# First K by the plain queue beside first Q by the cast queue, and weights in two column halves, in a planned attention and FFN kernel

## The chip, the cores and the metric

The kernel runs on one core of a Trainium2 chip. The core has five engines that work side by side, each through its own list of instructions in a fixed order: TensorE (PE, matmul), VectorE (DVE), ScalarE (ACT), GpSimd (POOL) and SyncE (SP). SP, ACT and POOL also issue DMAs, which 16 DMA engines shared by all of them carry out. The metric is the device time of one execution in microseconds (us), the median over several runs. All runs and traces here are of one core.

## The reference

Block-sparse attention over 4 batches and 8 heads, 768 positions, 64 wide, and then a gated FFN over the 3,072 tokens:

```python
scores = q @ k.T / sqrt(64)            # per batch and head, 768 x 768
mask   = |block_i - block_j| <= 1, first and last block row and column,
         and 3 sampled key blocks for each query block   # blocks of 32
attn   = softmax(where(mask, scores, -1e9))
x      = (attn @ v), heads side by side                  # 3072 x 512
gate   = sigmoid(x @ w_gate)                             # 512 x 1536
out    = (gate * (x @ w_val)) @ w_out                    # 1536 x 512
```

All inputs are float32 in HBM (the sampled blocks are integers), and the output is float32. The kernel computes in float16 with float32 sums.

## The kernel before

The work is cut into 12 tiles n of 256 query tokens: batch b = n // 3 and chunk c = n % 3. The 8 heads go in 4 pairs p. For each (n, p) there are three score groups of 256 keys each: `attend` (L546) makes the transposed scores on PE (L560), the exponential on ACT (L575, 128 x 1024 in one instruction), and the mask. Tile 0 adds the mask as a bias on PE (the other half of L560); later tiles multiply by a 0/1 mask on DVE (L583). Then 24 matmuls with V (L598) give the values and, through a column of ones, the row sums. DVE takes the reciprocal (L606) and scales (L609), and the result x is transposed, for the first three tiles on PE (L634, copied by DVE at L639), for later ones by a DMA of SP (L622).

When all four pairs of a tile are there, `ffn` (L648) runs over 12 blocks f of 128 hidden columns: 4 matmuls with w_gate and 4 with w_val (L660), a tanh on ACT (L679), and a product on DVE (L686). After the 12 blocks, L704 multiplies with w_out, ACT or DVE evacuates y (L721, L717), and SP stores it (L726).

Inputs of batch 0 come by POOL's queue, which casts float32 to float16 on the way: `load_half` (L396), and `turn_pe` (L402) transposes K and Q on PE (L410), DVE copying the result (L414). Q is loaded for all heads at once, first the third that tile 0 needs (`qc0`), and last the other two thirds (`qc12`). The order is K0, qc0, K1, V0, K2, V1, K3, V2, V3, qc12. The weights follow in POOL's queue: gate and value in column blocks 0-256, 256-512, 512-1024 and 1024-1536 (L457), then w_out in three pieces (L466). Batches 1 to 3 come by SP's queue as float32: `load` (L357, L362) for K, Q and V of one pair; ACT or DVE casts them (`cast_qk`, L391 or L393; `cast_v`, L382 or L384), and `turn_dma` (L418) has SP transpose K and Q (L424). Three staging buffers each for K, Q and V (`ks`, `qs`, `vs`) bound how far these loads run ahead. Those of batch 1 wait for the second piece of w_out.

Nothing of this order is dynamic on the chip. A planner, class `Plan`, takes every operation with an engine (or two, for casts), a duration, its buffers and a priority, plays the whole kernel through in Python with these durations, and at each step gives a free engine the ready operation of the lowest priority number. The order that comes out is what each engine's list holds. The planner knows DMAs by the line `dma_free = max(dma_free, now + 2.1) + o.dma`, landing 0.2 later. Where a DMA comes later on the chip than in the plan, the engine that stands in front of its data waits, and with it all that is behind it in its list. While PE has nothing to do in the plan before 22 us, it gets matmuls on zeros (L347, the "spin").

## Time and profile before

| | us |
|---|---|
| median of 5 runs | 302.55 |
| lowest and highest | 300.15 and 302.87 |
| the profiled execution, its own time | 300.15 |
| span of its trace | 298.4 |
| first exponential (L575) begins | 9.24 |
| first FFN matmul (L660) begins | 26.87 |
| last store begins after y of | 295.18 |
| PE, ACT, DVE busy | 288.8, 211.8, 192.6 |

The span is the time from the first to the last instruction; some 1.75 us of the execution's own time lie around it. The granted TensorE clock is full throughout. The profiled execution is the lowest of the five runs, so what is worked out from its trace is set against 300.15 first, and against the median after that.

DMAs from issue to landing, as the list of DMA issues gives them (the size is that of the destination; a casting DMA reads twice as much):

| what | queue | KB | issue to landing, us |
|---|---|---|---|
| table e (issued at 0.74) | SP | 192 | 2.3 |
| K of pair 0 (issued at 1.24) | POOL | 192 | 4.0 |
| qc0 (issued at 2.04) | POOL | 256 | 4.7 |
| qc12 (issued at 7.89) | POOL | 512 | 9.6 |
| gate and value, 512 columns | POOL | 512 | 12.9 to 15.8 |
| w_out, three pieces | POOL | 512 | 16.9 to 19.3 |
| K, Q, V of batches 1 to 3 | SP | 384 | 5.4 to 5.6 (medians) |

How to read the profile: a row of the timeline has the start, the time from start to end, the engine, the source line, the operation, what it writes and reads, and how many instructions were merged; in brackets stands the idle time of the engine before it and what ended it. PEld is the load of weights into PE, beside the matmuls. PEq, SPq and the like are the sequencers, which issue DMAs and wait. The chain of waits is followed back from the last instruction; its rows have the start, the length and what decided in that time.

### The profile page before, as it was taken

The page shows a single profiled execution, that of the slowest core. Times are in us where ns is not written, and L with a number is a line of the kernel's source. Part 1 is how long each engine was busy: PE and PEld are TensorE (multiplying, and loading weights), DVE is VectorE, ACT ScalarE, POOL GpSimd, SP SyncE. Part 2 cuts the span into 40 slices and gives each one's busy share as a digit, 9 for nine tenths or more (in the row PEclk, how much of TensorE's full clock was granted, in tenths as well). Part 3 has the DMA queues.
Part 4 walks back from the last instruction along what each step waited for, and adds up shares of the span by engine and source line. Part 5 has one row for each costly group of instructions (what it writes and reads, how often), then busy time and mean ns, then how long its engine had stood idle before and what let it go on. Part 6 is the DMA issues. An engine that isn't in the chain of part 4 may idle for free.

```text
span 298.4 us, 8114 instructions
## 1 busy us (share of the span) xinstructions
PE 288.8 (97%) x3407; PEld 211.1 (71%) x3407; DVE 192.6 (65%) x448; ACT 211.8 (71%) x328; POOL 16.0 (5%) x25
## 2 busy tenths in 40 slices
PE   8898998999999899999999999999999999999995
PEld 6676874776687478578578677768768767778673
DVE  3769868788777687576667567756656756635230
ACT  1789795998887878788678578678578578434331
POOL 8750000000000000000000000000000000000000
PEclk9999999999999999999999999999999999999999
DMA  9999999999979957460210210120120120120101
GB/s 122 193 198 207 206 267 309 307 306 285 266 176 237 299 181 104 106 159 3 64 46 0 53 58 1 29 81 0 29 81 0 29 82 1 29 81 0 38 35 70
DMA packets 53420, 35.36 MB, mean 119 GB/s; under 512 B 32136, under 2 KB 50440, under 8 KB 53384
## 3 DMA queue, kind: packets, MB, share of 16 engines
q1 hardware_dynamic: 43248, 27.77, 35.7%
q0 software_dynamic: 10064, 7.08, 16.0%
q8 instruction: 26, 0.43, 0.7%
q14 instruction: 10, 0.08, 0.1%
q10 hardware_dynamic: 72, 0.01, 0.0%
HBM read 28.55 MB, written 6.29 MB: 117 GB/s over the span
## 4 chain that ended last, share of the span: by engine, by line
PE 74%; DMA 16%; POOL 3%; SPq 2%; ACT 2%; DVE 1%; issue 1%; POOLq 0%
PE psum L660 38%; PE psum L704 18%; PE psum L560 9%; PE psum L598 9%; DMA wo<-in_moe_w_out_dram 6%; DMA wv<-in_moe_w_val_dram 4%; DMA vs<-in_v_dram 3%; DMA ks<-in_k_dram 2%; SPq L362 1%; DMA qs<-in_q_dram 1%; ACT pt L575 1%; POOL k L398 1%; POOL q L398 1%; POOL qc L398 1%; DVE pt L583 0%
## 5 line engine op out<-in xcount | busy, mean ns | idle before, releaser
L575 ACT ACTIVATE pt<-psum 128x1024 f16<-128x1024 f32 x144 | 143.3, 1024 | 34.8 <-PE psum L560 34.7
L583 DVE TENSOR_TENSOR pt<-pt,mask 128x1024 f16<-128x1024 f16 x132 | 90.5, 690 | 49.2 <-ACT pt L575 48.9
L660 PE MATMUL psum<-x,wg 128*128 128x256 f16 x576 | 86.7, 273 | 1.2 <-DMA x<-x 0.8
L660 PE MATMUL psum<-x,wv 128*128 128x256 f16 x576 | 86.7, 273 | 0.0
L686 DVE SCALAR_TENSOR_TENSOR h<-tg,psum 128x256 f16<-128x256 f32 x144 | 56.6, 415 | 19.0 <-ACT tg L679 18.8
L679 ACT ACTIVATE tg<-psum 128x256 f32<-128x256 f32 x144 | 55.2, 388 | 16.9 <-PE psum L660 13.1
L704 PE MATMUL psum<-wo,h 128*128 128x512 f16 (+1 forms) x300 | 66.6, 371 | 0.0
L660 PEld LDWEIGHTS <-wv 128*128 128x128 f16 x576 | 53.7, 98 | 12.9 <-issue 7.1
L660 PEld LDWEIGHTS <-wg 128*128 128x128 f16 x576 | 54.8, 98 | 10.6 <-issue 3.5
L704 PEld LDWEIGHTS <-h 128*128 128x128 f16 x300 | 27.6, 98 | 30.7 <-issue 3.6
L560 PE MATMUL psum<-qT,kT 64*128 64x256 f16 x576 | 47.8, 271 | 1.5 <-ACT pt L575 1.5
L598 PEld LDWEIGHTS <-pt 128*128 128x128 f16 x1152 | 41.0, 97 | 5.0 <-issue 1.6
L598 PE MATMUL psum<-v,pt 128*128 128x65 f16 x1152 | 42.8, 193 | 0.5 <-DVE pt L583 0.4
L560 PEld LDWEIGHTS <-kT 64*128 64x128 f16 x576 | 23.5, 94 | 16.5 <-issue 13.4
L721 ACT ACTIVATE y<-psum 128x512 f32<-128x512 f32 (+1 forms) x21 | 12.1, 577 | 23.4 <-PE psum L704 21.7
L609 DVE TENSOR_TENSOR x<-psum,rz 128x256 f16<-128x256 f32 x48 | 20.3, 424 | 1.7 <-DVE rz L606 0.2
L606 DVE RECIPROCAL rz<-psum 128x4 f32<-128x4 f32 x48 | 8.5, 177 | 13.5 <-PE psum L598 13.1
L393 ACT CAST q<-qs 128x768 f16<-128x768 f32 x7 | 5.8, 832 | 5.1 <-DMA qs<-in_q_dram 5.1
L391 DVE CAST k<-ks 128x768 f16<-128x768 f32 x8 | 4.5, 557 | 4.4 <-DMA ks<-in_k_dram 4.4
L384 ACT CAST v<-vs 128x768 f16<-128x768 f32 x7 | 5.8, 834 | 1.3 <-PE psum L598 1.0
L560 PE MATMUL psum<-bias,e 64*128 64x256 f16 x48 | 6.4, 272 | 0.1
L532 DVE TENSOR_SCALAR mask<-psum 128x512 f16<-128x512 f32 x9 | 6.0, 685 | 0.3
(40 smaller groups left out, 70.8 us busy)
## 6 DMA issues: line engine op xcount, KB each, us to landing
out_dram<-y SPq DMA_DIRECT2D x23, 256.0 KB, 2.3
ks<-in_k_dram SPq DMA_DIRECT2D x12, 384.0 KB, 5.4
qs<-in_q_dram SPq DMA_DIRECT2D x12, 384.0 KB, 5.6
vs<-in_v_dram SPq DMA_DIRECT2D x12, 384.0 KB, 5.5
wo<-in_moe_w_out_dram POOLq DMA_DIRECT2D x3, 512.0 KB, 18.1
wg<-in_moe_w_gate_dram POOLq DMA_DIRECT2D x2, 512.0 KB, 14.3
wv<-in_moe_w_val_dram POOLq DMA_DIRECT2D x2, 512.0 KB, 14.9
k<-in_k_dram POOLq DMA_DIRECT2D x4, 192.0 KB, 5.5
```

What stands on the lines that cost most here:

```text
L398: landed[nm] = nc.gpsimd.dma_start(t(), src[nm][0][:, hs, js])
L560: nc.tensor.matmul(st()[:, hd, jj * CH : (jj + 1) * CH], l[r, 2 * tt + jj, :], m[r, 2 * c : 2 * c + 2, :], start=not (own and masked), sto ...
L575: lambda st=st, pt=pt: nc.scalar.activation(pt().rearrange("p h j q -> p h (j q)"), st(), AF.Exp, scale=SCALE),
L583: nc.vector.tensor_tensor(t, t, mask()[:, c, tt].unsqueeze(1).to_broadcast([128, 2, 512]), op=ALU.mult)
L598: nc.tensor.matmul(o()[:, 2 * jq + hd, 0:65], pts[j // 2]()[:, hd, j % 2, jq * 128 : jq * 128 + 128], v_[:, hd, j, 0:65], start=(j == 0), ...
L606: P.op("DVE", 0.2, lambda: nc.vector.reciprocal(rz(), o()[:, :, 64:65]), reads=[o], writes=[rz], prio=seq - 5)
L609: lambda: nc.vector.tensor_tensor(x16().rearrange("p j (h d) -> p (j h) d", d=64), o()[:, :, 0:64], rz().to_broadcast([128, 4, 64]), op=AL ...
L660: nc.tensor.matmul(t()[:, z : z + w], wt()[:, i, f * 128 : (f + 1) * 128], xT[g, i]()[:, 0:w], start=(i == 0), stop=(i == NP - 1),)
L679: lambda tg=tg, a=pair[0]: nc.scalar.activation(tg()[:, 0:w], a[0]()[:, a[1] : a[1] + w], AF.Tanh, scale=0.5),
L686: lambda tg=tg, a=pair[1], h_=h_: nc.vector.scalar_tensor_tensor(h_()[:, 0:w], tg()[:, 0:w], 1.0, a[0]()[:, a[1] : a[1] + w], op0=ALU.add, ...
L704: nc.tensor.matmul(py()[:, m], hts[g, f]()[:, tt * 128 : (tt + 1) * 128], wo()[:, f, m], start=(f == 0), stop=(f == NF - 1),)
L721: lambda py=py, y=y, m=m: nc.scalar.activation(y()[:, m], py()[:, m], AF.Copy, scale=0.5),
```

## The change

The change does the following.

- K of pair 0 of batch 0 is loaded by SP in float32, as SP's first DMA, ahead of the table e, and ACT casts it into a buffer of its own. The identity goes from SP's queue to ACT's.
- POOL's queue loads Q by pairs, whole, in the order of `FIRST`: Q0, K1, Q1, K2, Q2, V0, K3, Q3, V1, V2, V3. The transposes of Q still come in two parts, the third for tile 0 first and the rest before tile 1.
- Gate and value weights come in two halves of 768 columns.
- K, V and Q of pair 0 of batch 1 (the last entry of `HALF`) also come by POOL's casting queue, between the value weights and w_out, and are transposed on PE.
- SP's loads of batch 1 (now pairs 1 to 3) wait for the third piece of w_out instead of the second; a load also stands behind the transposes of earlier pairs (`turned`).
- The planner's constants for DMAs are others: 1.9 (SP, ACT) or 2.6 (POOL) to the first byte, 0.3 at the end, more per load, and a `slack` that is added to a landing (0.3 or 1.3 for casting loads, 1.5 for SP's loads). POOL begins at 0.55.
- Score groups of `attend` are kept in order (`scored`), and the building of the masks is tied to points in the attention (`behind`), with its DVE part at a lower priority number.

```diff
+EDGES = [0, 768, 1536]
+FIRST = [
+    ("q", 0), ("k", 1), ("q", 1), ("k", 2), ("q", 2), ("v", 0), ("k", 3), ("q", 3), ("v", 1), ("v", 2), ("v", 3),
+]
+HALF = [(0, 0), (0, 1), (0, 2), (0, 3), (1, 0)]
...
+        free["POOL"] = 0.55
...
-                    dma_free = max(dma_free, now + 2.1) + o.dma
-                    o.seen = dma_free + 0.2
+                    first = now + (2.6 if e == "POOL" else 1.9)
+                    if o.dma > 0.15:
+                        first = dma_free = max(dma_free, first) + o.dma
+                    o.seen = first + 0.3 + o.slack
...
+    P.op("ACT", 0.4, lambda: nc.scalar.dma_start(ident16(), id_h.ap()), writes=[ident16], prio=-88, dma=0.1)
...
-        writes=[e24], prio=-92, dma=0.5,
+        writes=[e24], prio=-94.5, dma=0.5,
...
-    P.op("SP", 0.5, lambda: nc.sync.dma_start(ident16(), id_h.ap()), writes=[ident16], prio=-91, dma=0.3)
...
+    def load_half(nm, b, p, prio, dur=0.72):
+        c = sb(f"{nm}16" if nm != "v" else "vh", [128, 2, NJ, 64], f16)
+        half16[nm, b, p] = stage[nm, b, p] = c
+        o = P.op(
+            "POOL", dur, lambda: nc.gpsimd.dma_start(c(), src[nm][b][:, 2 * p : 2 * p + 2]),
+            writes=[c], prio=prio, dma=1.28,
+        )
+        o.slack = 0.3 + b
+        return o
...
+    load("k", 0, 0, -95)
+    t, c = stage["k", 0, 0], one([128, 2, NJ, 64], f16, "k16_first")
+    half16["k", 0, 0] = c
+    P.op("ACT", 0.83, lambda t=t, c=c: nc.scalar.copy(c(), t()), reads=[t], writes=[c], prio=-67)
+    for i, (nm, p) in enumerate(FIRST):
+        last_in = load_half(nm, 0, p, -60 + i, 0.82 if i == 0 else 0.72)
     for p in range(NP):
...
+        turn_pe("k", 0, p, every, -40 + 2 * p)
+        turn_pe("q", 0, p, early, -39.5 + 2 * p)
+        cast_v(0, p, -30 + p)
...
-    edges = [0, 256, 512, 1024, 1536]
+    edges = EDGES
...
+    next_in = [w_in["v", NF - 1]]
+    for p in range(NP):
+        if (1, p) in HALF:
+            for nm in "kqv":
+                next_in.append(load_half(nm, 1, p, -31 + p))
     for s in range(3):
-        load_out(s, -30 + s, w_in["v", NF - 1])
+        load_out(s, -20 + s, next_in)
...
-                writes=[st], prio=seq, mode="row",
+                writes=[st], prio=seq, mode="row", behind=scored[-1:],
...
             for p in range(NP):
-                turn_pe(
-                    qc12, 2 * p, tr["q", 0, p], slice(2, NJ), 2.0
-                )
-            for c_, pr in ((1, 11.5), (2, 13.5), (0, 26)):
-                build_mask(c_, pr)
+                turn_pe("q", 0, p, later, 9.0, [valued[0, 1]])
+            build_mask(1, 11.5, [valued[0, 0]])
+            build_mask(2, 13.5, [valued[0, 2]])
+            build_mask(0, 26, xT[0, NP - 1].writers[-1:])
...
+                if (b + 1, p) in HALF:
+                    for nm in "kq":
+                        turn_pe(nm, b + 1, p, every, 3 * NP * (3 * b + 2))
+                    cast_v(b + 1, p, 3 * NP * (3 * b + 2))
+                    continue
                 for nm in "kqv":
-                    if b == 0:
-                        load(nm, b + 1, p, seq + p, after=[w_out[4]], sync="o")
-                    else:
-                        load(nm, b + 1, p, seq + p)
+                    o = load(
+                        nm, b + 1, p, seq + p, behind=turned[:-2][-2:],
+                        **(dict(after=[w_out[8]], sync="o") if b == 0 else {}),
+                    )
+                    o.slack = 1.5
                 for nm in "kq":
-                    turn_dma(nm, b + 1, p, seq + p + CAST_LATE * b)
+                    turned.append(turn_dma(nm, b + 1, p, seq + p + CAST_LATE * b))
```

## The prediction

> **What bounds the kernel now.** I read five views, in this order. First the page, for the share of each engine:
>
> ```profile
> span 298.4 us, 8114 instructions
> PE 288.8 (97%) x3407; PEld 211.1 (71%) x3407; DVE 192.6 (65%) x448; ACT 211.8 (71%) x328; POOL 16.0 (5%) x25
> DMA  9999999999979957460210210120120120120101
> ```
>
> PE looks full and the DMA row is full for the first third. A busy PE is not a PE at its peak, so the second view is the chain of waits, whose pieces on PE give what an instruction costs when nothing holds it, and whose other pieces show the places where something else decides:
>
> ```profile
> 9.52 10.61 DMA wv<-in_moe_w_val_dram
> 20.13 0.28 issue
> 20.42 18.10 DMA wo<-in_moe_w_out_dram
> 38.53 0.43 SPq L362
> ...
> 43.14 8.88 DMA vs<-in_v_dram
> ...
> 98.77 6.69 DMA ks<-in_k_dram
> 105.48 0.56 DVE k L391
> ...
> 145.79 0.76 PE psum L598 x24
> 146.55 0.54 PE psum L560 x8
> 147.09 2.70 PE psum L704 x12
> ...
> 263.79 13.97 PE psum L660 x128
> ```
>
> From the last four: 0.032 us for a value matmul, 0.068 for a score matmul, 0.22 for an output matmul (wo), 0.109 for a gate or value-weight matmul. The third view, the busy time by stage and by line, counts these instructions in each stretch. Count times price is work done; the rest of the stretch is PE time lost:
>
> - 0 to 5.3: only filler matmuls on zeros; 5.3 lost.
> - 5.3 to 26.87 (first FFN matmul): 100 transposes at 0.028 (12 start within about 0.33) 2.8, 120 score matmuls, most of them masked (two start each 0.11), at about 0.058 7.0, 96 value matmuls 3.1, 18 mask matmuls at 0.11 2.0, the rest 0.7: 15.6 of 21.6; 6.0 lost.
> - 26.87 to 44.27: 16.5 of 17.4; 0.9 lost.
> - 44.27 to 55.3: 24 output 5.3, 24 score 1.6, 48 value 1.5, 6 transposes 0.3: 8.7 of 11.0; 2.3 lost.
> - 89.66 to 109.48: 58 gate 6.3, 24 output 5.3, 40 score 2.7, 96 value 3.0: 17.3 of 19.8; 2.5 lost.
> - elsewhere after 55 the chain runs from PE piece to PE piece, until 3.2 at the end.
>
> So the kernel is bound by PE from about 27 us on, with three holes: the fill, 44 to 55, and 90 to 109. Only these can be won back. The fourth view, the timeline, shows what makes them:
>
> ```profile
> 9.24 4.69 ACT L575 ACTIVATE pt<-psum 128x1024 f16<-128x1024 f32 x5 [6.24 <-PE psum L560]
> ...
> 45.09 0.56 DVE L382 CAST v<-vs 128x768 f16<-128x768 f32 x1 [0.88 <-DMA vs<-in_v_dram]
> 45.57 0.42 DVE L609 TENSOR_TENSOR x<-psum,rz 128x256 f16<-128x256 f32 x1
> ...
> 47.86 0.83 ACT L393 CAST q<-qs 128x768 f16<-128x768 f32 x1 [3.07 <-DMA qs<-in_q_dram]
> ```
>
> The fill: the first exponential runs at 9.24, and from there ACT is the bound, 1.024 us for each of the 12 of tile 0; it has only about 1.9 us of gaps until 24.5. The FFN cannot begin before tile 0 is done. The second hole: casts of batch 1 stand in DVE's and ACT's fixed order before work that is ready, and wait for their DMA: the scaling of x at 45.57 had its reciprocal at 42.80. The third hole is the same mechanism (DVE waits 1.8 for ks at 105.48). The fifth view, DMA issues, gives landings: k for pair 0 4.0 after its issue at 1.24, so 5.24; then about 1.16 per 384 KB of float32 source; last q piece 17.45; 512-column weights about 2.6 apart (1 MB each); wo at 36.0, 38.5, 41.1.
>
> **What the Trainium skill says.** Perfetto Trace Analysis, section Identifying the Most-Contended Engine, says that matmul occupancy is no measure of closeness to the limit, since matmuls are pipelined. The trace agrees: PE is 97% busy and still loses the 17 us above. DMA: Bandwidth & Descriptors, section Issuing engines are not separate DMA queues, says that DMAs from several engines share the same 16 DMA engines, so that issuing from two saves issue time alone. It follows that K beside Q does not double the rate; the trace before has no such pair of large loads at its start. The same page, section Specifications, gives about 1 us to the first byte for POOL's queue and 0.6 for SP's. The trace agrees in sign: 192 KB from SP landed after 2.3, 192 KB (twice that at the source) from POOL after 4.0, of which 0.81 was the issue.
>
> **The change part by part.**
>
> *Start.* K of pair 0 leaves SP at 0.74 instead of POOL at 1.24, ahead of the e table, as float32; ACT casts it (0.83, from the ACT cast rows). 384 KB more source than e needs: about 2.3 + 0.5 after 0.74 is 3.6 at best, 4.2 with sharing; cast done by 5.0, its 12 transposes and copy (0.56) by 6.3. ACT's three small issues and the 1.28 table load end near 3.5, so they hide. Q of pair 0 is now POOL's first: 5.24 if K is out of its way, 6.3 if K goes wholly ahead (one load's 1.1). I take 5.8. Four transposes and a 0.27 copy: first score 6.4; before, 0.66 from first score to first exponential: 7.05. Against 9.24 that is 2.2 earlier. Bounds 1.2 and 2.9. In before the first score stood behind pair 1's K (landed 7.94) in PE's order; now one third of it precedes it. Later pairs land 2.3 apart (K and Q), exponentials of a pair take 3.07, so ACT is not starved; V of pair 0 lands near 11.5, when ACT has scores in hand.
>
> *Weights in two halves.* The bytes are the same, 6.3 MB at about 400 GB/s by the landings, 15.7 us from about 17. First gate half 21, first value half 24.8 (26 at the low end of the rates), second 28.8 and 32.7. Before, two blocks were usable at 20.1; now six at 24.8. In the new order of PE, eight score groups of tile 1 stand before the first value-weight matmul; with 2.2 gained it comes at 26 (28.08 before). Block 6 stands at 34 to 35 by the same count. So the coarser halves cost 0 as long as the lead is 2.2; if the rate falls to that of the K loads (340 GB/s), they cost 1 to 2. Fewer instructions on POOL save nothing: its issue waits already lie under a full queue.
>
> *Batch 1, pair 0, by the cast queue.* Three loads ahead of wo: wo ends 3.3 later, near 44 (41.1 before). First output matmul stands near 46.8, so nothing, or 1 if wo slips to 47.6. It takes two SP transposes and three casts out of the order and adds 24 PE transposes: 24 x 0.028 = 0.7 on PE, which nothing hides. K lands near 34, Q near 36; PE meets them after 36.
>
> *Later loads.* Pairs 1 to 3 of batch 1 wait for the last wo piece (44) instead of the second (38.5). But the orders of ACT and DVE now put all 36 exponentials of batch 0 before the first of these casts (28 before). The work ahead of it takes PE to about 54, so the casts find their data; the hole at 44 to 55 shrinks. I take 1.6 of its 2.3. The same added allowance for landing, and loads held behind the transposes of two pairs back, act on the hole at 90 to 109. I can't replay that stretch: between nothing and all of 2.5; I take 1.2. New waits on SP queue output stores and x transposes behind a load; y has three buffers, so I price it at 0, with 1 as the bad end.
>
> Masks move within DVE's slack (it is busy 3.5 to 4 of each 5 us up to 25), and filler matmuls fill PE only where it would stand. I price both at 0, 0.3 either way.
>
> Sum: -2.2 - 1.6 - 1.2 + 0.7 = -4.3. The profiled execution took 300.15 (span 298.4), so 295.85 (span 294.1). It was the fastest of the five; the median is 2.4 above it. That spread looks like late DMAs, which the new order should tolerate partly: I add half, 1.2. Forecast 297.0.
>
> **Rivals.**
>
> - *Only the start is won.* The casts of batch 1 stall at new places, as the loads are now denser after 44. For it: the chain has DMAs at 44 to 52 and 98 to 105. Against: the order of the casts. 300.15 - 2.2 + 0.7 = 298.65, as a median 299.9.
> - *All three holes close.* 300.15 - 2.2 - 2.3 - 2.5 + 0.7 = 293.85, as a median 295.1.
> - *Slower: the late gate.* Pairs 1 to 3 of batch 1 start at 44, and each needs two SP transposes that take 3.13 and 2.78 beside loads (44.21 and 47.44 before), 6 a pair. If PE's order meets their scores sooner, PE stands: 3 for each of the first two pairs, 1 for the third, and SP's later loads shift with it. 300.15 - 2.2 + 0.7 + 7 = 305.65, as a median about 306. It decides once pair 1 is turned later than about 60; PE's order has some 5 us of FFN work between the last score of batch 0 and pair 1. Against: the casts need 44 + 4 + 1, turned by 56.
> - *The start does not come:* K and Q share the engines and both land after 6.5, the first value half after 27: gain gone, about 302.5.
>
> **How the numbers follow.** The forecast 0.55, only the start 0.18, all holes 0.12, the late gate 0.10, no start 0.05. The range 293.5 to 301.5 holds the first three with their bounds and leaves out nearly all of the last two. A measurement here tells 0.5% (1.5 us: 301.0 and 304.1) from no change. Faster: most of the first three, 0.81; same 0.08; slower 0.11.
>
> **What would show it.** The start: first exponential near 7.0 and first value-weight matmul near 26. Weights: no wait of that line for wv at block 0 or 6. Gate: the first SP load of batch 1 near 44, the output matmuls no later than 47, and no cast row with a DMA wait of 1 us or more between 44 and 60. Wrong: a PE wait for qT or kT between 52 and 75, or a first exponential after 8.

## The result and the profile after

The changed kernel takes 300.21 us (median of 43 runs, 297.59 to 301.81), the kernel before 301.1 us on the same chip (80 runs, 298.68 to 303.8). The ratio is 0.9966, with a 95% interval of 0.9953 to 0.9978: 0.3% faster, where 1.8% was forecast. The profiled execution of the changed kernel, at 297.59, was the fastest of its 43, and that of before, at 300.15, was faster than its median too. What the two traces show is therefore not yet what the medians show, and much of what follows comes from this. Ratios leave out the executions in a slower state of the chip, one of them at 478 us.

The page of the changed kernel, its span and PE's row:

```profile
span 295.8 us, 8172 instructions
PE 289.4 (98%) x3443; PEld 210.8 (71%) x3443; DVE 193.0 (65%) x450; ACT 211.6 (72%) x327; POOL 15.6 (5%) x25
```

The chain of waits of the changed kernel (start, length, what decided), at its start and in the two stretches where before had DMAs in it:

```profile
0.74 0.66 ACTq L337
1.42 2.72 DMA mi<-bb_mdet_iota
7.19 0.54 PE psum L582 x8
...
42.92 1.31 PE psum L683 x12
44.23 0.54 PE psum L582 x8
45.43 0.87 PE psum L683 x8
46.63 0.87 PE psum L621 x24
47.49 1.31 PE psum L683 x12
49.35 0.97 PE psum L727 x4
...
101.69 2.73 PE psum L683 x24
104.41 0.76 PE psum L621 x24
105.17 0.54 PE psum L582 x8
```

No DMA is left in it at 44 to 52 or at 98 to 105. The only one is the small table mi, at the very start. In the timeline of the changed kernel the first loads and what they lead to look like this:

```profile
3.98 0.83 ACT L451 CAST k_first<-ks 128x768 f16<-128x768 f32 x1 [0.54 <-DMA ks<-in_k_dram]
4.25 0.22 DVE L509 TENSOR_TENSOR eqs<-mi,sbi 24x72 f32<-24x72 f32 x1 [2.99 <-DMA mi<-bb_mdet_iota]
5.12 0.49 PE L523 MATMUL psum<-e,mb 24*128 24x256 f16 x2 [0.64 <-DVE mb L516]
5.61 0.53 PE L427 MATMUL psum<-ident,k_first 128*64 128x128 f16 x12
...
7.78 6.68 ACT L598 ACTIVATE pt<-psum 128x1024 f16<-128x1024 f32 x7 [2.97 <-PE psum L582]
...
28.00 0.61 PE L683 MATMUL psum<-x,wv 128*128 128x256 f16 x4
```

K of pair 0 lands at 3.98, 1.3 earlier than before, but its transposes begin at 5.61, and before at 5.31. In PE's fixed order the bias matmul (L523) stands ahead of them; it waits for mi, and mi lands 0.76 later than before (4.25 against 3.49). The first exponential still comes 1.46 earlier (9.24 to 7.78), but the first value-weight matmul stands where it stood (28.08 to 28.00). What stands just ahead of it, in before (first line) and in the changed kernel:

```profile
24.55 3.77 ACT L575 ACTIVATE pt<-psum 128x1024 f16<-128x1024 f32 x4 [0.24 <-PE psum L560]
...
22.93 5.71 ACT L598 ACTIVATE pt<-psum 128x1024 f16<-128x1024 f32 x6 [0.39 <-PE psum L582]
27.67 0.39 PE L582 MATMUL psum<-qT,kT 64*128 64x256 f16 x4 [0.16 <-ACT pt L598]
```

In both, ACT works through exponentials until this matmul is reached, and in the changed kernel the last score group ahead of it waits for one of them. The casts of batch 1, in the timeline of the changed kernel:

```profile
53.03 0.55 DVE L400 CAST k<-ks 128x768 f16<-128x768 f32 x1
54.25 0.83 ACT L402 CAST q<-qs 128x768 f16<-128x768 f32 x1
55.24 0.84 ACT L393 CAST v<-vs 128x768 f16<-128x768 f32 x1
```

None of the three has a bracket with a wait; before, the cast of Q had idled ACT for 3.07.

For all traces I count PE time lost as the prediction does: the length of a stretch, less the matmuls that start in it times their slot price. 44 to 110 us holds the second and third hole. Times in us; "half rate" is the stretch in which the matmuls of the scores, bias matmuls with them, take 0.39 to 0.42 from start to end instead of 0.27. "Again" is a second execution of the same program; the variants in the lower rows are described in the next section.

| trace | first exponential | first wv matmul | half rate | lost 0-44 | lost 44-110 | last output matmul |
|---|---|---|---|---|---|---|
| before | 9.24 | 28.08 | none | 12.6 | 6.4 | 294.87 |
| before, again | 11.46 | 31.03 | 10.4-14.3 | 15.3 | 6.3 | 297.89 |
| changed | 7.78 | 28.00 | none | 12.9 | 2.5 | 291.65 |
| changed, again | 10.02 | 31.35 | 9.0-12.4 | 16.1 | 2.4 | 295.00 |
| planning alone | 10.57 | 28.82 | none | 13.3 | 3.5 | 292.74 |
| planning alone, again | 9.77 | 28.32 | none | 12.9 | 4.0 | 292.75 |
| landing model alone | 11.57 | 30.74 | 10.5-13.4 | 15.2 | 3.5 | 294.80 |
| changed and filler | 7.91 | 28.14 | none | 13.0 | 2.5 | 291.79 |
| changed and more filler | 8.46 | 28.68 | none | 13.5 | 2.5 | 292.33 |
| planning and filler | 9.44 | 27.43 | none | 13.3 | 2.5 | 291.54 |

Three things stand in it. The holes of the changed kernel are smaller by 3.9 than those of before, in both pairs of traces. PE's half rate, which comes and goes between executions of one kernel, goes with 1.9 to 3.2 us more lost in the fill. And the first exponential can be compared within one order of instructions only. Changed, "changed and filler" and "changed and more filler" have the same order on PE, but for the filler. Their first exponentials begin 0.13 and 0.68 later than that of the changed kernel, and their last output matmuls 0.14 and 0.68 later: there the start arrives in full. Before and changed have different orders, and there 1.46 shrank to 0.08 by the first value-weight matmul.

### The profile page after: what moved, and what is told of

It is laid out like the page before. It is cut to its first block, busy times and chain, and to the rows that moved or that the text cites. A ratio compares the mean times of both kernels' runs of the same rounds, so it can differ in the third digit from the quotient of the medians.

```text
span 295.8 us, 8172 instructions
## 1 busy us (share of the span) xinstructions
PE 289.4 (98%) x3443; PEld 210.8 (71%) x3443; DVE 193.0 (65%) x450; ACT 211.6 (72%) x327; POOL 15.6 (5%) x25
## 3 DMA queue, kind: packets, MB, share of 16 engines
q0 software_dynamic: 7504, 7.47, 15.3%
## 4 chain that ended last, share of the span: by engine, by line
PE 95%; ACT 1%; DMA 1%; issue 1%; DVE 0%; ACTq 0%; DVEq 0%
PE psum L683 44%; PE psum L727 22%; PE psum L582 14%; PE psum L621 13%; PE psum L427 2%; ACT pt L598 1%; DMA mi<-bb_mdet_iota 1%; PE psum L356 1%; PE psum L657 1%; ACTq L337 0%; PE psum L544 0%; PE psum L523 0%; ACT y L744 0%; DVE mb L516 0%; DVE eqs L509 0%
## 5 line engine op out<-in xcount | busy, mean ns | idle before, releaser
L709 DVE SCALAR_TENSOR_TENSOR h<-tg,psum 128x256 f16<-128x256 f32 x144 | 57.0, 415 | 20.6 <-ACT tg L702 20.2
L727 PE MATMUL psum<-wo,h 128*128 128x512 f16 (+1 forms) x300 | 68.0, 371 | 0.0
L702 ACT ACTIVATE tg<-psum 128x256 f32<-128x256 f32 x144 | 55.4, 389 | 17.3 <-PE psum L683 13.6
L727 PEld LDWEIGHTS <-h 128*128 128x128 f16 x300 | 26.9, 98 | 29.3 <-issue 4.4
L744 ACT ACTIVATE y<-psum 128x512 f32<-128x512 f32 (+1 forms) x18 | 10.3, 574 | 22.3 <-PE psum L727 22.3
L629 DVE RECIPROCAL rz<-psum 128x4 f32<-128x4 f32 x48 | 8.6, 179 | 12.6 <-PE psum L621 11.7
L393 ACT CAST v<-vs 128x768 f16<-128x768 f32 x10 | 8.3, 838 | 0.3 <-PE psum L621 0.3
L356 PE MATMUL psum<-zero 128*128 128x128 f16 x51 | 5.6, 277 | 1.0 <-DVE zero L335 1.0
L740 DVE TENSOR_SCALAR y<-psum 128x512 f32<-128x512 f32 x7 | 4.8, 688 | 2.1 <-PE psum L727 1.9
## 6 DMA issues: line engine op xcount, KB each, us to landing
wg<-in_moe_w_gate_dram POOLq DMA_DIRECT2D x2, 768.0 KB, 13.6
```

The lines of the kernel that those rows point to most:

```text
L356: "PE", dur, lambda: nc.tensor.matmul(t(), zero(), zero(), start=True, stop=True),
L629: P.op("DVE", 0.2, lambda: nc.vector.reciprocal(rz(), o()[:, :, 64:65]), reads=[o], writes=[rz], prio=seq - 5)
L702: lambda tg=tg, a=pair[0]: nc.scalar.activation(tg()[:, 0:w], a[0]()[:, a[1] : a[1] + w], AF.Tanh, scale=0.5),
L709: lambda tg=tg, a=pair[1], h_=h_: nc.vector.scalar_tensor_tensor(h_()[:, 0:w], tg()[:, 0:w], 1.0, a[0]()[:, a[1] : a[1] + w], op0=ALU.add, ...
L727: nc.tensor.matmul(py()[:, m], hts[g, f]()[:, tt * 128 : (tt + 1) * 128], wo()[:, f, m], start=(f == 0), stop=(f == NF - 1),)
L744: lambda py=py, y=y, m=m: nc.scalar.activation(y()[:, m], py()[:, m], AF.Copy, scale=0.5),
```

## The experiments

Every ratio is to the kernel before on the same chip in the same session. The letters of the theories in the expectations hold within one group of experiments only. My first theory was that the start had become unsteady because the small tables land beside large loads; the rivals were the weight halves, the gate, and the first K itself.

**The two kernels again.** No edit.

> The changed kernel once more, nothing edited. Its profiled execution of 297.6 us was the fastest of 43, the median is 300.2. Theory A (late DMAs): a slower execution shows PE lost in front of a late load between 27 and 110 us, 1 to 3 us more than the 1.3 + 0.7 + 0.6 + 0.7 + 0.6 of the first trace, at the clock 1.00. Theory B (clock): a slower execution shows the same waits but a granted clock under 0.995, some 2 us of 298, late in the span. Ratio to before 0.9966 again.

> The kernel before once more, nothing edited, to see a second execution in a trace. Theory A: the lost PE time at 44 to 56 (2.5 us) and 90 to 110 (2.8 us) differs by a us or more from the first trace, and the total follows it. Theory B: the same holes, and a difference that stands in the granted clock.

Changed: 299.91, ratio 0.9946 (0.9926 to 0.9967). Before: 303.16 in a single run. Neither theory fits the changed kernel: between 44 and 110 it loses 2.4 the second time and 2.5 the first, and its clock is 1.00. What differs is the start. In the changed kernel again (timeline):

```profile
5.33 0.82 PE L523 MATMUL psum<-e,mb 24*128 24x256 f16 x2 [0.85 <-DVE mb L516]
6.41 0.85 PE L427 MATMUL psum<-ident,k_first 128*64 128x128 f16 x12 [0.26 <-DMA ident<-bb_ident]
...
9.13 0.42 PE L582 MATMUL psum<-qT,kT 64*128 64x256 f16 x2
```

mi came only 0.2 later, yet the first exponential 2.2 later: the same bias matmul takes 0.82 instead of 0.49, the twelve transposes 0.85 instead of 0.53. They also waited 0.26 for the identity table, which landed 0.8 later after its issue than in the first trace. PE runs at half rate, while the granted clock of this trace is 1.00. In before again the half rate is there too, but so is a late landing: PE waits 1.48 for the first Q, whose transposes began at 6.94 in the first trace.

```profile
8.36 0.85 PE L410 MATMUL psum<-ident,qc 128*64 128x128 f16 x12 [1.48 <-DMA qc<-in_q_dram]
```

And here the clock does tell. For the first 20 us, before again first and changed again second, the rows give the length, PE's busy time with its instructions, the granted clock, the DMA engines' busy share and GB/s:

```profile
0.00:20.00 20.00, 16.52 (x225) 0.83 1.20 166
0.00:20.00 20.00, 17.90 (x225) 1.00 1.09 186
```

In all these traces the clock reads 1.00 as long as the full rate has not come yet, though PE is at half rate; so a clock that is full throughout does not rule out a slow start. Only where the full rate is lost again does it read 0.50, from 7.7 to 14.5 in before again.

**Weights in four blocks, gate on the second piece.** Each undoes one part.

```diff
-EDGES = [0, 768, 1536]
+EDGES = [0, 256, 512, 1024, 1536]
```

> The changed kernel with the weights in the four old column blocks (256, 256, 512, 512). If the halves held back the start of the FFN (first value-weight matmul at 28.00, no earlier than before), this starts it 1 to 2 us sooner and the whole is 1 us faster. If the order of PE and the exponentials in front of it hold it, first value-weight matmul within 0.5 us of 28.0 and the total within 0.3%.

0.9939 (0.9911 to 0.9966): not told apart from the changed kernel (0.9946), so no cost of the halves is seen, and no gain. A difference under some 1 us would not be seen.

```diff
-            if s == 2:
+            if s == 1:
...
-                        **(dict(after=[w_out[8]], sync="o") if b == 0 else {}),
+                        **(dict(after=[w_out[4]], sync="o") if b == 0 else {}),
```

> The changed kernel with the SP loads of batch 1 waiting for the second piece of w_out again. If late loads of batch 1 cost the changed kernel its gain in most executions, 1 to 2 us faster at the median. If not, within 0.3%, with the loads starting near 40 instead of 43.

0.997 (0.995 to 0.9989): not told apart from the changed kernel, and no faster. The first SP load of batch 1 left at 41.27 instead of 42.96. The late gate, my slower rival, shows no cost.

**Where the tables and the first K come from.** The first variant only makes the planner expect mi 2 us later, so that it fills longer and puts the bias matmul behind the transposes; the second issues mi and e by SP ahead of K; the third mi ahead of K, and e by ACT; the fourth gives K of pair 0 back to the cast queue, ahead of Q.

```diff
+    late.slack = 2.0
...
+    P.op("SP", 0.5, lambda: nc.sync.dma_start(mi(), mi_h.ap()), writes=[mi], prio=-97, dma=0.1)
...
-    load("k", 0, 0, -95)
+    load_half("k", 0, 0, -61, 0.82)
```

> The changed kernel with the planner told that table mi lands 2.0 us later, so that about a dozen more filler matmuls on zeros stand before the bias matmul. Theory C (a pause of PE in front of the bias matmul puts its clock at half, matmuls of 0.42 instead of 0.27 us, for about 7 us): no pause, no 0.42 us score matmuls, first exponential between 8 and 8.5 every time, median some 1 us below the changed kernel. Theory D (only the late table counts): the same or slower by the added filler.

> The changed kernel with mi and e issued by SP ahead of K of pair 0. Theory D (mi and e land late because they share the DMA engines with K and Q loads): mi is there by 3.5 as before, bias done by 5.8, K lands about 0.9 later, first exponential near 7.5 and without the swing; median 1 to 2 us below the changed kernel. Theory C alone: the pause before the bias matmul goes too, since mi comes sooner, so the same gain, but the pause then moves to K.

> The changed kernel with mi first on SP, then K, and e on ACT's queue behind the sampled blocks. Theory D: mi by 3.2, K as in the changed kernel (3.9 to 4.3), e decides; first exponential 7 to 7.5 if e lands by 4.8, later where e is late. Median between the changed kernel and the one with both tables first, or better than both.

> The first part of the change undone alone: K of pair 0 comes by the casting queue again, first of it, Q second; the rest as changed. If the two queues side by side are what delays the tables, mi and e land as before (3.5 and 3.1), but Q of pair 0 lands near 6.5; first exponential near 8.5 and steadier. If the median is the same as that of the changed kernel within 0.3%, the plain queue for K has won nothing.

In order: 1.0007 (0.9983 to 1.0031), 0.9951 (0.9924 to 0.9978), 0.9974 (0.9948 to 0.9999), 0.9944 (0.9924 to 0.9965). With mi by SP, its first user starts at 2.34, but K, issued 0.4 to 0.8 later, then lands 4.0 to 5.6 after its issue instead of 3.2, so the tables' gain is K's loss. The last ratio says most: without the part that the change is named for, the kernel is as fast as with it. Its trace also settles what made mi late: with K back in the cast queue mi has its first user at 3.35, as in before. The first exponential is then at 9.44. The tables are late because of K beside Q, but they are not what costs the forecast gain, and my first theory fell. The first variant came out slower although its trace (298.15, span 296.4) is its best execution; why the median is worse the trace doesn't show.

**What closes the holes.** Two variants take parts from the changed kernel: the half-precision pair of batch 1, then the slack and order of the plain loads.

```diff
-HALF = [(0, 0), (0, 1), (0, 2), (0, 3), (1, 0)]
+HALF = [(0, 0), (0, 1), (0, 2), (0, 3)]
```

> The changed kernel, but pair 0 of batch 1 is loaded by the plain queue and turned by the DMA again, like the other pairs; all else as changed. Theory A (the holes closed because the loads of batch 1 are planned with later landings, so the pair itself matters little): the 24 extra transposes go, PE loses at most 1.5 us between 44 and 56 us, ratio to before 0.992 to 0.997. Rival (the hole at 44 to 56 is closed by this pair alone, which needs neither SP load nor cast): 2 us or more are lost again in that stretch, less 0.7 for the transposes, ratio 0.999 to 1.003.

0.9936 (0.9913 to 0.9959), in time alone; no trace of it is used.

```diff
-                        nm, b + 1, p, seq + p, behind=turned[:-2][-2:],
+                        nm, b + 1, p, seq + p,
...
-                    o.slack = 1.5
+                    o.slack = 0.0
```

> The changed kernel with the planner's slack of the plain loads at 0 instead of 1.5 us and without their order behind earlier transposes: casts and transposes of batches 1 to 3 are again placed as if loads landed early. Theory A: PE waits come back, 1.5 to 3 us lost in 90 to 110 us and perhaps 0.5 to 1 in 130 to 200, ratio 1.000 to 1.006. Rival (the hole closed because the half-precision pair moved every later load ahead): nothing comes back, 0.7 us or less lost in 90 to 110, ratio 0.994 to 0.998.

0.9949 (0.9931 to 0.9966), 2.4 lost in 44 to 110: no hole comes back. The slack and order are not what closes them. For the pair it is the time alone that says so: the rival had 0.999 to 1.003.

The third gives the kernel *before* only the planner's new model of landing and the slack and order of plain loads. First loads, tables, weight blocks and gate stay as they were.

```diff
-                    dma_free = max(dma_free, now + 2.1) + o.dma
-                    o.seen = dma_free + 0.2
+                    first = now + (2.6 if e == "POOL" else 1.9)
+                    if o.dma > 0.15:
+                        first = dma_free = max(dma_free, first) + o.dma
+                    o.seen = first + 0.3 + o.slack
...
+                    o.slack = 1.5
```

> The kernel before with one part of the change: the planner's new model of landing, the slack of 1.5 us on plain loads, and plain loads behind earlier transposes. First loads, tables, weights in four blocks, gate on the second output weight piece: as before. Theory A (planning alone closes the holes, and the start of the kernel before is no worse): first exponential near 9.2 to 11.5 as before, holes at 44 to 56 and 90 to 110 shrink from 5.3 us together to under 2.5, ratio 0.988 to 0.995, so at least as fast as the changed kernel. Rival (the holes close only with the new order of loads): 4 us or more still lost in the two stretches, ratio 0.998 to 1.003.

297.22 us, 0.987 (0.9846 to 0.9895): four times the gain of the whole change. Its chain of waits:

```profile
20.90 18.42 DMA wo<-in_moe_w_out_dram
...
40.32 7.06 DMA vs<-in_v_dram
47.40 0.56 DVE v L385
...
98.99 1.83 PE psum L707 x8
101.59 0.87 PE psum L601 x24
102.45 0.88 PE psum L663 x8
103.33 0.54 PE psum L563 x8
103.87 2.29 PE psum L663 x20
```

The hole at 98 to 105 is gone from the chain; that at 44 is smaller (1.6 lost in 44 to 56, 2.5 before) but still there. Then the model of landing alone, without slack and order:

> The kernel before with nothing but the planner's new model of when a transfer lands: no slack on the plain loads, no order of loads behind earlier transposes. Theory A1 (the model of landing closes the holes: transfers no longer queue up behind each other's fixed cost): under 3 us lost in 44 to 56 and 90 to 110 together, ratio 0.985 to 0.991, as with slack. Rival A2 (the slack of 1.5 us, which keeps casts and transposes away from the landing, closes them): over 4 us still lost there, ratio 0.997 to 1.003.

0.9934 (0.99 to 0.9968), between the two forecasts, but the trace decides for the model: 1.3 lost in 44 to 56 and 0.8 in 90 to 110. By its constants a plain load alone is planned to land 3.27 after its issue (1.9, 1.07 and 0.3) and by the old ones 3.32 (2.1, 1.02 and 0.2), a casting load 0.6 later than by the old ones. Each further load in a row adds 1.07 instead of 1.02. So the model closes most of the holes while it gives plain loads hardly more time. Which of its parts does it was not run. What the trace loses against planning alone is lost before 18 us, where both programs issue the same instructions.

**PE's half rate.** These two traces, of the same instructions for 41 us, are the cleanest pair for it. Planning alone (timeline):

```profile
4.99 0.49 PE L506 MATMUL psum<-e,mb 24*128 24x256 f16 x2
5.56 0.53 PE L413 MATMUL psum<-ident,k 128*64 128x128 f16 x12
...
9.46 0.53 PE L413 MATMUL psum<-ident,k 128*64 128x128 f16 x12 [1.38 <-DMA k<-in_k_dram]
9.92 0.28 PE L563 MATMUL psum<-bias,e 64*128 64x256 f16 x2
10.04 0.27 PE L563 MATMUL psum<-qT,kT 64*128 64x256 f16 x2
```

The model of landing alone (timeline):

```profile
5.05 0.81 PE L506 MATMUL psum<-e,mb 24*128 24x256 f16 x2
5.80 0.85 PE L413 MATMUL psum<-ident,k 128*64 128x128 f16 x12
...
9.71 0.85 PE L413 MATMUL psum<-ident,k 128*64 128x128 f16 x12
10.50 0.40 PE L563 MATMUL psum<-bias,e 64*128 64x256 f16 x2
10.68 0.42 PE L563 MATMUL psum<-qT,kT 64*128 64x256 f16 x2
```

One trace runs at twice the rate of the other. The first Q lands 1.2 later in the second trace (8.68 against 7.44), but the first trace then waits for K of pair 1, so both are level at 9.5 to 9.7. The second trace stays at half rate until 13.4, and its first value-weight matmul comes 1.9 later. The Trainium skill, TensorE: Matmul & The Clock Gate, Part 1 on the HAM clock gate, says that the half rate is PE's default, that it ends after a window of about 3.4 us of sustained activity, and that the window runs free of the program, so that the end varies from run to run. The traces agree on the default and on the variation: the filler on zeros starts every 0.107 us at first in all of them, and full rate shows first at 3.6 to 6.3 in some, at 8.5 to 13.6 in others. The late ones do not fit 3.4 us: PE has been at work from 0.99, and with K back in the cast queue it worked until 8.5 with no pause over 0.06 before the full rate came. Why it comes so late there is open. In four traces (before again, four weight blocks, tables first, first K on planning) it begins before 7.5 and is lost again for 3.4 to 6.8 us, after pauses of PE.

The mean granted clock of each execution counts this second form: it is 0.988 to 0.993 in those four traces and 0.997 or more in all others, and 3.4 us at 0.50 make a mean of 0.994 over 298 us (an estimate from the length of these stretches). By that mark full rate was lost again in 124 of 147 executions of before, 25 of 62 of the changed kernel, 3 of 12 of planning alone and none of the 20 of the three kernels with filler below. But it does not set the medians: in the changed kernel these executions are 0.5 us slower at the median than its others in one set and 0.9 faster in the other. The late first full rate can't be counted so.

So filler was put where PE waits: twelve zero matmuls ahead of the first bias matmul of the changed kernel.

```diff
+                [
+                    nc.tensor.matmul(pb()[:, 0], zero(), zero(), start=True, stop=True)
+                    for _ in range(12 if c == 0 else 0)
+                ],
```

> The changed kernel in its own order, with 12 matmuls of zeros put directly in front of the first bias matmul, so that PE runs while it would wait for the transposes' data. Theory B (a pause of PE in the first 8 us lets it run at half rate for some 7 us in most executions, which the changed kernel's profiled execution escaped): no score of 0.36 us or more in the profile, ratio 0.985 to 0.992. Rival (the start is set by when tables and loads land, and the half rate is the lesser part): ratio 0.994 to 0.998, first exponential between 8 and 10 with or without slow matmuls; the filler itself can cost up to 0.7 us.

298.51 us, 0.9915 (0.9889 to 0.9941): at the upper end of the theory's range, and clear of the 0.9953 to 0.9978 of the unedited kernel, though not of the 0.9926 to 0.9967 that it had the second time. The timeline:

```profile
4.07 0.83 PE L525 MATMUL psum<-zero 128*128 128x128 f16 x12
5.31 0.49 PE L528 MATMUL psum<-e,mb 24*128 24x256 f16 x2 [0.41 <-DVE mb L516]
5.74 0.53 PE L427 MATMUL psum<-ident,k_first 128*64 128x128 f16 x12
```

mi is no earlier than in the first trace of the changed kernel, the full rate is there at 4, and the first exponential comes at 7.91. That is no better than the first trace of the changed kernel (7.78): what the filler gains lies in the other executions. Their median is 0.8 above the profiled one here, and was 2.6 above it without filler. Later I added eight more ahead of the first Q transposes:

> The changed kernel with 12 matmuls of zeros in front of the first bias matmul and 8 in front of the first Q transposes. Theory D: at least as good as with 12 alone (0.9915), ratio 0.986 to 0.992, no slow score after 9 us. Rival: no better than the changed kernel unedited, 0.994 to 0.998.

298.92 us, 0.9906 (0.9871 to 0.9941), eight runs within 0.9 us of each other; no half rate after 5 us in its trace. The same on planning alone, eight in front of the first Q transposes and ten in front of K of pair 1, beside planning alone once more:

> Planning alone once more, unedited. Its first 45 us of instructions are those of the model of landing alone, yet the one had 0.987 and a profile with PE at full rate from 4.99 us, the other 0.993 and a profile at half rate until 13.4 us. Theory D (the planning gain holds; what differs between the two is when PE leaves its half rate, by chance): ratio between 0.985 and 0.994, first exponential 8.5 to 11.6, holes at 44 to 56 and 90 to 110 under 3 us together. Rival (the slack itself is worth 2 us): ratio under 0.989 again.

> Planning alone with 8 matmuls of zeros in front of the first Q transposes and 10 in front of the second K transposes, where PE waits for loads. Theory D: more activity in the first 9 us lets PE leave its half rate by about 9 us at the latest and not fall back, ratio 0.002 to 0.005 below that of h1 in this call, profile without slow scores after 10 us. Rival (landings set the start): no difference, or up to 0.8 us slower where the data is there before the zeros are done.

Planning alone again: 297.21, 0.9857 (0.9808 to 0.9907). With filler: 296.81, 0.9845 (0.9801 to 0.9888), the fastest kernel of all, but not told apart from planning alone: the gap of 0.001 is less than expected, and the two traces of planning alone have no half rate to lose after 5 us. Planning alone stays under 0.989, as the rival said that gives the slack 2 us, but 0.9857 lies in the theory's range too, so it decides nothing between them.

**Which part spoils the planning's gain.** Once from each side. First, planning alone plus the part that the change is named for (first K by SP and ScalarE's cast, first Q at the head of the cast queue, identity by ACT):

```diff
+        if p == 0:
+            load("k", 0, 0, -95)
+            t = stage["k", 0, 0]
+            P.op("ACT", 0.83, lambda t=t, c=c: nc.scalar.copy(c(), t()), reads=[t], writes=[c], prio=-67)
```

> Planning alone (0.987) plus the part the change is named for: first K by the plain queue with a cast on ScalarE, first Q at the head of the cast queue, identity table on ScalarE's queue; V stays between K, weights in four blocks. Theory C1 (this start is what costs the changed kernel its gain): tables land after 4 us, first exponential no earlier than 9.5 in the profile, ratio 0.991 to 0.997. Rival C2 (the loads are as good as before's and the loss comes from the order of work in the fill): first exponential 1 to 2 us earlier than the 10.57 of planning alone, ratio 0.980 to 0.987.

0.9933 (0.9904 to 0.9962): these loads, with the order of work that the planner makes of them, cost about 0.6% against planning alone. The timeline:

```profile
4.38 0.22 DVE L497 TENSOR_TENSOR eqs<-mi,sbi 24x72 f32<-24x72 f32 x1 [3.13 <-DMA mi<-bb_mdet_iota]
7.36 0.64 PE L413 MATMUL psum<-ident,qc 128*64 128x128 f16 x16 [2.24 <-DMA qc<-in_q_dram]
8.31 0.51 PE L511 MATMUL psum<-e,mb 24*128 24x256 f16 x2
```

The planner put Q's transposes first; PE waits 2.24 for them, and the bias matmul and K's transposes stand behind. The first exponential is at 12.56, later than without the part. Second, the changed kernel with before's first loads:

```diff
-    for i, (nm, p) in enumerate(FIRST):
-        last_in = load_half(nm, 0, p, -60 + i, 0.82 if i == 0 else 0.72)
+        load_some(c, "k", hs, slice(0, NJ), -60 + 2 * p, 1.02)
+        if p == 0:
+            load_some(qc0, "q", slice(0, H), slice(0, 2), -59.5, 1.5)
...
+    last_in = load_some(qc12, "q", slice(0, H), slice(2, NJ), -50, 2.6)
```

> The changed kernel with the first loads of before: first K at the head of the cast queue, a third of Q of all heads beside it, V between K, the rest of Q last; the e table alone in front on the plain queue. Planning, fill order, weight halves, half-precision pair and late gate stay as changed. Theory C1 (the first loads cost the gain): ratio 0.985 to 0.990, like planning alone. Rival C2 (the fill's new order of work costs it): ratio 0.993 to 0.998, like the changed kernel, with 19 us or more between the first exponential and the first value-weight matmul, where planning alone takes 18.3.

0.993 (0.99 to 0.9959): the gain of planning alone does not come back, so the first loads alone are not what the changed kernel lost. The new order of work in the fill, the rival, is the likelier cause but not shown: 18.97 us from the first exponential to the first value-weight matmul, at the edge of what it expected, in a trace that is at half rate from 10.1 to 12.7. The three traces of one order above speak for it too: from the first exponential to the first value-weight matmul they take 20.2 each, before 18.8, planning alone 18.3 to 18.6.

## Why the forecast was too large

The forecast was 297.0, the result 300.21. Of the 3.2 between them, 1.7 lie in the profiled execution (297.59, where 295.85 was forecast) and 1.4 in its distance to the median (2.6, where 1.2 was allowed). The baseline moved too: five runs of before gave 302.55, eighty give 301.1. The rival "only the start is won" named 299.9, close to the result, but by luck: it won the start and kept the holes, and the runs show the reverse.

**The start, -2.2: this step failed.** The first exponential came 1.46 earlier in the profiled execution, and nothing of it arrived: the fill lost 12.9 instead of 12.6, and the first value-weight matmul stood at 28.00, where 26 was forecast. That the first exponential moves everything behind it was right, within one order of instructions: filler that made it 0.13 and 0.68 later made the end 0.14 and 0.68 later. The step failed in carrying the lead over to another order. It set "26" as 28.08 less 2.2, though it had seen that eight score groups of tile 1 stand in front of this matmul in the new order; in before there are six (80 and 72 score matmuls in the traces, 4 to a group, 12 groups of them tile 0). ACT bounds this stretch. In it 19 exponentials begin instead of 18, 0.92 to 0.94 apart in a row, and ACT's waits add up to 2.30 instead of 1.87 (the brackets in its timeline). (The prediction priced each at 1.024.) Together that is nearly all of the 1.38 by which the stretch from the first exponential to this matmul grew, from 18.84 to 20.22, and the lead of 1.46 is used up.

K's own lead was gone before its first use: it landed 1.3 earlier, its cast takes 0.83, and its transposes, behind a table of 4.5 KB that had not been on the path before, began 0.30 later than in before. What the first exponential gained fits Q at the head of the cast queue: with K put back in front of Q it is at 9.44. The section of the Trainium skill that the prediction cited, Issuing engines are not separate DMA queues (DMA: Bandwidth & Descriptors), says that loads of several engines interleave on the same DMA engines. The traces agree: mi has its first user 2.8 after its issue beside K and Q on two queues, and 2.0 after it where K is in the cast queue.

**The spread of the start was mis-sized.** The prediction set its sum against one profiled execution, put the spread down to late DMAs and allowed 1.2 for it; the median lies 2.6 above. Late landings are in the spread (1.48 for the first Q in before again), but the larger term in the table is PE's half rate, with 1.9 us in the cleanest pair. At the last output matmul the changed kernel is ahead by 3.2 in the traces without half-rate scores (294.87 and 291.65) and by 2.9 in those with them (297.89 and 295.00). The medians differ by 0.9 only: the changed kernel's lies 2.6 above its first trace, before's 1.0 above its own. Something takes more from the usual execution of the changed kernel than from that of before. That it is the half rate is inferred, as these executions have no trace. Filler in the changed kernel, which changes nothing else, fits it: it is worth 0.3 to 0.6% (0.9915 and 0.9906 against 0.9946 and 0.9966) and takes the median to within 0.7 to 0.8 of the profiled execution. The variant that only made the planner fill longer did not gain, though, so filler as such is not the cure.

**The holes, -1.6 and -1.2: right in kind, too small.** They closed by 1.8 (44 to 56) and 2.2 (90 to 110), and 3.9 from 44 to 110 in all. The planning of landings is what closes most of them: alone on the kernel before, with slack and order, it takes 2.4 to 2.9 off, without them 2.9. The order of casts that the prediction named for the hole at 44 is there: the 36th exponential begins at 53.34, ACT's first cast of a plain load at 54.25. The added allowance for landing and the loads held behind transposes, which it named for the other, are not needed: both holes stay small without them, under a model that gives plain loads hardly more time than the old one.

**Extra transposes, +0.7.** The traces have 24 more, 0.7 at their slot price. With +0.3 in the fill, -3.9 in the holes and -0.3 after 110 that gives the -3.2 by which the last output matmul moved. As lost time is what these prices leave over, the sum must balance; it is no test of the price. Of the 3.2, 0.6 went again behind the last output matmul: the span is 2.6 shorter. **Weight halves, gate, masks at 0:** no run shows a cost of halves or gate, and none takes the masks apart. The first SP load of batch 1 left at 42.96 (44 forecast), and the late-gate rival fell. Its median, by the same 1.2 as the others, should have read 306.9 and not 306.

**What stays open.** Planning alone has a median of 297.2, the changed kernel with filler 298.5 and 298.9, though their profiled spans are 296.2 and 295.9 to 296.5. The 1.3 us or more between them lie in executions that have no trace: the profiled ones of planning alone are 0.8 slower than its medians, those with filler in the changed kernel 0.7 to 0.8 faster. Nor is it shown why planning with slack has a median 2 us below planning without it, when the first 41 us have the same instructions and the holes are equal. How often the first full rate comes late in each kernel was not counted.

## What to carry to other kernels

An earlier first result is worth only what still stands at the next point where engines meet. Within one order it arrived to the end (0.68 of 0.68); under a new order a lead of 1.46 was used up by one more exponential and its waits. So count, in the new order, what stands in front of that point, and don't take the old time less the lead. Where a schedule is planned ahead, the planning of landings can be worth more than faster loads: model, slack and order together gave 1.3 to 1.4%, four times the whole change, and the model alone 0.7%. And before a start is tuned, look whether PE is at half rate in the traces, by the spacing of its matmuls as well as by the clock, and compare two executions of the same program first.

## What was not expected of the hardware

- PE at half rate for up to 13.6 us of a 300 us kernel. The granted clock reads 1.00 while full rate has not come yet, and 0.50 when it is lost again (four traces). Two programs with the same first instructions differ by 1.9 us at the first value-weight matmul.
- Full rate lost again at 7.1 in the trace with four weight blocks, after two pauses of PE of 1.0 and 0.7 us.
- A plain load of 384 KB lands 3.2 us after an issue at 0.74, but 4.0 after 1.18 and 5.6 after 1.57, when the cast queue has begun at 1.23.
- A table of 4.5 KB was ready for its first user at 3.49 before, at 4.25 to 6.56 beside K and Q in the changed kernel and its variants with the same tables, at 3.35 with K back in the cast queue, and at 2.34 when issued ahead of K.
